# Dense–SiLU–dense on one core: first chunk by DMA transpose with the contraction outermost over eight PSUM banks, row-tiled tails, one SiLU activation

## The chip, the core and the metric

The kernel runs on one core of a Trainium2 chip. The metric is device time in microseconds (us) of one execution, median over the runs that were timed. Lower is better.

## What is computed

```python
B, S, D, F = 1, 2048, 640, 1728        # x: (B,S,D)  w1: (D,F)  w2: (F,D), all bf16
h = jnp.einsum("bsd,df->bsf", x, w1)
h = h * sigmoid(h)                     # silu
out = jnp.einsum("bsf,fd->bsd", h, w2)
```

Both products contract over the partition dimension of 128: D = 640 is five slices (`DT = 5`), F = 1728 is thirteen full slices and a tail of 64. The first product needs x transposed (D on the partitions), the second needs h with F on the partitions, which is how the first one writes it.

## The kernel before, in words

The instructions of each engine are written out by hand in their order; semaphores tie the engines together. The sequence is cut into four chunks of 512 rows (`SCH`, `NSC`).

**Getting x transposed.** Chunk 0 is loaded as it lies, half by SP (L206) and half by ACT (L401), and turned on TensorE: 20 matmuls of 128x128 against an identity that POOL builds (L184 to L196), L295, whose results VectorE and ScalarE copy from PSUM to `xT_sb` (L468, L416). Chunks 1 to 3 are transposed by the DMA engines on the way in, five transposes of 512x128 per chunk, issued by SP (L224). SP issues nothing of these before the first half of x has landed (wait ahead of L213) and the third group of w1 has landed (wait ahead of L224). w1 comes in four groups of columns (L406 on ACT, L213 on SP), w2 in four pieces on SP after chunk 2's transposes (L233, L236, L243).

**Warm-up.** TensorE multiplies zeros nine times, 512 columns each (L277), while the first data is on its way.

**First product.** A unit is one chunk by one slice of F: five matmuls of 512 columns, one for each slice of D, into one of four PSUM banks (`ps1`, L350). The first two slices of chunk 0 are split into halves of 256 columns. ScalarE writes the sigmoid of a unit to SBUF (L426), VectorE multiplies it with the unit in PSUM and writes `hT_sb` (L490). The tail of 64 columns of F is done for two chunks at a time (L339): the two matmuls of a pair write partitions 0 to 63 and 64 to 127 of one bank, and the result goes to the matching half of slice 13 of `hT_sb` (L481). POOL clears that slice first (L198), so the other half of it is zero.

**Second product.** For each of 16 tiles of 128 rows, all 14 slices of F, the 14th being the half-filled tail at full height: one matmul of 512 columns and one of 128 for each slice (L388), into two pairs of banks in turn (`ps2`). VectorE copies the 512 columns out (L503), ScalarE the 128 (L438), SP stores the tile (L259). The last two tiles are done together so that the last step is the narrow one: VectorE copies 1024 columns (L515), ScalarE 256 (L450), with stores by SP (L265) and ACT (L455).

Of the kernel before, what the change touches and what calls it, by code (L numbers as in the profile page):

```python
# [6 lines left out]
ALU = mybir.AluOpType  # L7


def bass_standalone__dense_activation_silu__prompt_kernel(  # L10
# [14 lines left out]
    assert D % P == 0 and S % 512 == 0 and 512 < D <= 1024  # L25
    DT = D // P
    FT = (F + P - 1) // P
    FP = FT * P
    F_LAST = F - (FT - 1) * P
    ST = S // P  # L30
    SCH = 512
    NSC = S // SCH
    JB = SCH // P
    NB1 = 4
    NOB = 4
    DA = 512
    DB = D - DA
    assert ST >= 4 and ST % 2 == 0 and (ST - 2) % NOB + 1 == (ST - 1) % NOB
    assert JB % 2 == 0

    w1_groups = [(0, 2), (2, 4), (4, 8), (8, FT)]
    N_W1_ACT = 1
    W1_BIG = 2

    def w1_group_of(ft):
        for gi, (a, b) in enumerate(w1_groups):
            if a <= ft < b:
                return gi
        raise AssertionError

    HN = SCH // 2
    N_SPLIT_FT = 2
    units = []
    for ft in range(N_SPLIT_FT):
        units.append((0, ft, 0, HN))
    for ft in range(N_SPLIT_FT):
        units.append((0, ft, HN, HN))
    PACK_TAIL = (F_LAST <= 64) and (FT >= 2)
    FT_REG = FT - 1 if PACK_TAIL else FT
    for ft in range(N_SPLIT_FT, FT_REG):  # L60
        units.append((0, ft, 0, SCH))
    for sc in range(1, NSC):
        for ft in range(FT_REG):
            units.append((sc, ft, 0, SCH))
        if PACK_TAIL and sc % 2 == 1:
            units.append((-1, sc - 1, sc, 0))
    if PACK_TAIL and NSC % 2 == 1:
        units.append((-1, NSC - 1, None, 0))
    NU = len(units)

    def unit_chunks(u):
        if u[0] == -1:
            return [c for c in (u[1], u[2]) if c is not None]
        return [u[0]]

    dve_incs = [len(unit_chunks(u)) if u[0] == -1 else 1 for u in units]
    dve_val = []
    acc = 0
    for inc in dve_incs:
        acc += inc  # L80
        dve_val.append(acc)
    chunk_done_cnt = {}
    for i, u in enumerate(units):
        for c in unit_chunks(u):
            chunk_done_cnt[c] = dve_val[i]
    def tail_half(sc):
        if not PACK_TAIL:
            return 0
        if NSC % 2 == 1 and sc == NSC - 1:
            return 0  # L90
        return sc % 2

    n_w2_full = FT - 1 if F_LAST != P else FT
    w2_half = n_w2_full // 2
    n_w2_dmas = (4 if (F - (FT - 1) * P) <= 64 else 3) if n_w2_full != FT else 2
    N_INIT = 3 + (1 if (not PACK_TAIL and FP != F) else 0)
    N_PAD = 1 if (PACK_TAIL or FP != F) else 0
    N_WARM_MM = 9
    TPV = 3
    assert TPV <= 4 and DT - TPV <= 4  # L100

    TP_BANKS = {0: (1, 0), 1: (1, 8), 2: (0, 8), 3: (1, 0)}

    def tp_slot(j, dt):
        which, base = TP_BANKS[j % 4]
        slot = base + dt if dt < TPV else base + 4 + (dt - TPV)
        return which, slot

    with ExitStack() as es:
# [3 lines left out]
        def ps(name, shape, dtype):  # L113
            return es.enter_context(nc.psum_tensor(name, shape, dtype))

        def sem(name):
            return es.enter_context(nc.semaphore(name))

        xT_sb = sb("xT_sb", [P, DT, S], bf16)
        w1_sb = sb("w1_sb", [P, DT, FP], bf16)  # L120
        w2_sb = sb("w2_sb", [P, FT, D], bf16)
        hT_sb = sb("hT_sb", [P, FT, S], bf16)
        sig_sb = sb("sig_sb", [P, NB1, SCH], bf16)
        o_sb = sb("o_sb", [P, NOB, D], bf16)
        x0_sb = sb("x0_sb", [P, JB, D], bf16)
        ident = sb("ident", [P, P], bf16)
        warm_sb = sb("warm_sb", [P, 32], fp32)
        z_sb = sb("z_sb", [P, SCH], bf16)
        ps1 = ps("ps1", [P, NB1, SCH], fp32)
        ps2 = ps("ps2", [P, 2, 1024], fp32)  # L130
        tp_views = [
            ps1[:, :, :].rearrange("p a (k s) -> p (a k) s", s=P),
            ps2[:, :, :].rearrange("p a (k s) -> p (a k) s", s=P),
        ]

        sem_init = sem("sem_init")
        sem_w2pad = sem("sem_w2pad")
        sem_z = sem("sem_z")
        sem_x0 = [sem(f"sem_x0_{i}") for i in range(JB // 2)]
        sem_x = [None] + [sem(f"sem_x{i}") for i in range(1, NSC)]  # L140
        sem_w1 = [sem(f"sem_w1_{i}") for i in range(len(w1_groups))]
        sem_w2 = sem("sem_w2")
        sem_o = [sem(f"sem_o{i}") for i in range(NOB)]
        sem_tp = sem("sem_tp")
        sem_tpc_v = sem("sem_tpc_v")
        sem_tpc_a = sem("sem_tpc_a")
        sem_pe1 = sem("sem_pe1")
        sem_act1 = sem("sem_act1")
        sem_dve1 = sem("sem_dve1")
        sem_pe2 = sem("sem_pe2")  # L150
        sem_ev_v = sem("sem_ev_v")
        sem_ev_a = sem("sem_ev_a")
        sem_ofin = sem("sem_ofin")
        block = es.enter_context(nc.Block())

        w1_v = w1.rearrange("(dt p) f -> p dt f", p=P)
        x0_v = xf[0:SCH, :].rearrange("(j p) d -> p j d", p=P)
        w2_full_v = w2[0:n_w2_full * P, :].rearrange("(ft p) d -> p ft d", p=P)

        segs = []  # L160
        for st in range(ST - 2):
            b2 = st % 2
            segs.append([(st, 0, b2, 0, DA), (st, 1, b2, DA, DB)])
        sA, sB = ST - 2, ST - 1
        segs.append([(sA, 0, 0, 0, DA), (sB, 0, 0, 512, DA)])
        segs.append([(sA, 1, 1, 0, DB), (sB, 1, 1, 512, DB)])
        grp_order = []
        for seg in segs:
            for g in seg:
                grp_order.append((g[0], g[1]))  # L170
        grp_idx = {g: i + 1 for i, g in enumerate(grp_order)}
        seg_done_idx = {}
        for seg in segs:
            last = max(grp_idx[(g[0], g[1])] for g in seg)
            for g in seg:
                seg_done_idx[(g[0], g[1])] = last
        grp_loc = {}
        for seg in segs:
            for (st, ci, b2, c0, ncol) in seg:
                grp_loc[(st, ci)] = (b2, c0, ncol)  # L180

        @block.gpsimd
        def _(pool):
            pool.memset(z_sb[:, SCH // 2:SCH], 0.0).then_inc(sem_z, 1)  # L184
            pool.memset(ident[:, :], 0.0).then_inc(sem_init, 1)
            pool.wait_ge(sem_init, 1)
            pool.affine_select(
                out=ident[:, :],
                in_=ident[:, :],
                compare_op=ALU.not_equal,  # L190
                fill=1.0,
                base=0,
                pattern=[[-1, P]],
                channel_multiplier=1,
            ).then_inc(sem_init, 1)
            pool.memset(warm_sb[:, :], 0.0).then_inc(sem_init, 1)  # L196
            if PACK_TAIL:
                pool.memset(hT_sb[:, FT - 1, :], 0.0).then_inc(sem_w2pad, 1)  # L198
            elif FP != F:
                pool.memset(w1_sb[:, :, F:FP], 0.0).then_inc(sem_init, 1)  # L200
                pool.memset(w2_sb[:, FT - 1, :], 0.0).then_inc(sem_w2pad, 1)

        @block.sync
        def _(sp):
            hj = JB // 2
            sp.dma_start(  # L206
                out=x0_sb[:, 0:hj, :], in_=x0_v[:, 0:hj, :]
            ).then_inc(sem_x0[0], 16)

            def load_w1_group(gi):  # L210
                a, b = w1_groups[gi]
                f0, f1 = a * P, min(b * P, F)
                sp.dma_start(  # L213
                    out=w1_sb[:, :, f0:f1], in_=w1_v[:, :, f0:f1]
                ).then_inc(sem_w1[gi], 16)

            sp.wait_ge(sem_x0[0], 16)
            for gi in range(N_W1_ACT, len(w1_groups)):
                load_w1_group(gi)

            def x_chunk_transposes(sc):
                s0 = sc * SCH
                for dt in range(DT):
                    sp.dma_start_transpose(  # L224
                        out=xT_sb[:, dt, s0:s0 + SCH],
                        in_=xf[s0:s0 + SCH, dt * P:(dt + 1) * P],
                    ).then_inc(sem_x[sc], 16)

            sp.wait_ge(sem_w1[W1_BIG], 16)
            for sc in range(1, NSC):  # L230
                x_chunk_transposes(sc)
                if sc == min(2, NSC - 1):
                    sp.dma_start(  # L233
                        out=w2_sb[:, 0:w2_half, :], in_=w2_full_v[:, 0:w2_half, :]
                    ).then_inc(sem_w2, 16)
                    sp.dma_start(  # L236
                        out=w2_sb[:, w2_half:n_w2_full, :],
                        in_=w2_full_v[:, w2_half:n_w2_full, :],
# [308 lines left out]
```

## Time and profile before

| | |
|---|---|
| runs (us) | 130.3, 190.81, 131.05; median 131.05 |
| span of the profiled execution | 128.5 us |
| own time of the profiled execution | not given apart; the two near runs lie 1.8 and 2.5 us above its span |
| busy: TensorE, VectorE, ScalarE, POOL | 124.7, 52.1, 39.5, 2.8 us |
| DMA | 9.87 MB, mean 77 GB/s over the span |

The profile shows one execution. Line numbers (L388) are lines of the kernel before. The timeline and the chain give starts and durations in us from the start of the span; groups give the count, the busy time in us and the mean duration of one in ns. Matmuls are pipelined, so the mean duration of one is longer than the distance from one to the next; distances are had by dividing a stretch by its count. PE is TensorE, PEld its weight loads, DVE VectorE, ACT ScalarE, SPq and ACTq the DMA issues of SyncE and ScalarE.

### The profile page before, as it was taken

How to read it: one execution, taken by the hardware profiler on the slowest of the kernel's cores; microseconds unless marked ns; L12 is line 12 of the kernel's file. 1: busy time of each engine (PE TensorE's matmuls, PEld its weight loads, DVE VectorE, ACT ScalarE, POOL GpSimd, SP SyncE). 2: the span in 40 equal slices, each digit the busy share in tenths (PEclk: the TensorE clock that was granted, in tenths of full speed). 3: DMA queues.
4: the chain of work that ended last, by engine and by line, in shares of the span. 5: the costliest groups of instructions: out<-in, count | busy, mean ns of one | idle time of the engine just before them, and what ended most of it. 6: DMA issues, size and time to landing. Idle time of an engine off the chain costs nothing.

```text
span 128.5 us, 1884 instructions
## 1 busy us (share of the span) xinstructions
PE 124.7 (97%) x767; PEld 63.9 (50%) x767; DVE 52.1 (41%) x78; ACT 39.5 (31%) x77; POOL 2.8 (2%) x9
## 2 busy tenths in 40 slices
PE   6999999999999999999999999999999999999992
PEld 2574444444444444444455555555555555555461
DVE  0475666666676666666662210222220122221021
ACT  4355555555555555555520000000000000000001
POOL 7000000000000000000000000000000000000000
PEclk9999999999999999999999999999999999999999
DMA  3897463599900000000000111111011111011103
GB/s 100 258 367 207 109 96 87 98 355 347 195 8 5 0 3 0 0 0 0 0 5 15 36 51 51 56 51 48 3 51 51 56 51 51 12 39 56 51 0 102
DMA packets 15752, 9.87 MB, mean 77 GB/s; under 512 B 8832, under 2 KB 15744, under 8 KB 15744
## 3 DMA queue, kind: packets, MB, share of 16 engines
q1 hardware_dynamic: 14544, 9.03, 24.8%
q10 hardware_dynamic: 1200, 0.72, 1.8%
q8 instruction: 6, 0.10, 0.3%
q14 instruction: 2, 0.02, 0.0%
HBM read 5.16 MB, written 2.62 MB: 61 GB/s over the span
## 4 chain that ended last, share of the span: by engine, by line
PE 97%; ACT 1%; POOL 0%; issue 0%; POOLq 0%
PE ps L388 47%; PE ps L350 44%; PE ps L277 3%; PE ps L339 2%; PE ps L295 1%; ACT xT_sb L416 1%; ACT o_sb L450 0%; POOL z_sb L184 0%; POOLq L532 0%
## 5 line engine op out<-in xcount | busy, mean ns | idle before, releaser
L388 PE MATMUL ps<-w_sb,hT_sb 128*128 128x512 bf16 (+1 forms) x448 | 61.0, 299 | 0.0
L350 PE MATMUL ps<-xT_sb,w_sb 128*128 128x512 bf16 (+1 forms) x270 | 56.5, 371 | 0.0
L388 PEld LDWEIGHTS ps<-w_sb,hT_sb 128*128 128x128 bf16 x448 | 34.4, 98 | 26.8 <-issue 0.4
L490 DVE TENSOR_TENSOR hT_sb<-ps,sig_sb 128x512 bf16<-128x512 f32 (+1 forms) x54 | 36.3, 672 | 19.9 <-ACT sig_sb L426 19.4
L350 PEld LDWEIGHTS ps<-xT_sb,w_sb 128*128 128x128 bf16 x270 | 26.2, 98 | 29.9 <-issue 0.4
L426 ACT ACTIVATE sig_sb<-ps 128x512 bf16<-128x512 f32 (+1 forms) x56 | 32.6, 582 | 26.5 <-PE ps L350 25.3
L503 DVE CAST o_sb<-ps 128x512 bf16<-128x512 f32 x14 | 9.7, 692 | 42.3 <-PE ps L388 42.3
L438 ACT CAST o_sb<-ps 128x128 bf16<-128x128 f32 x14 | 3.7, 266 | 49.3 <-PE ps L388 49.3
L277 PE MATMUL ps<-z_sb 128*128 128x512 bf16 x9 | 3.4, 557 | 1.1 <-POOL z_sb L184 1.1
L468 DVE CAST xT_sb<-ps 128x384 bf16<-128x384 f32 x4 | 1.9, 549 | 4.1 <-PE ps L295 4.1
L515 DVE CAST o_sb<-ps 128x1024 bf16<-128x1024 f32 x1 | 1.2, 1225 | 5.4 <-PE ps L388 5.4
L481 DVE TENSOR_TENSOR hT_sb<-ps,sig_sb 64x512 bf16<-64x512 f32 x4 | 2.8, 689 | 1.1 <-ACT sig_sb L426 1.0
L450 ACT CAST o_sb<-ps 128x256 bf16<-128x256 f32 x1 | 0.4, 373 | 7.3 <-PE ps L388 7.3
L277 PEld LDWEIGHTS ps<-z_sb 128*128 128x128 bf16 x9 | 1.1, 136 | 2.9 <-issue 1.8
L339 PE MATMUL ps<-xT_sb,w_sb 128*64 128x512 bf16 x20 | 2.5, 384 | 0.0
L416 ACT CAST xT_sb<-ps 128x256 bf16<-128x256 f32 x4 | 1.3, 373 | 1.9 <-PE ps L295 1.9
L410 ACT ACT_TABLE_LOAD x1 | 1.3, 1283 | 1.8 <-issue 1.8
L198 POOL MEMSET hT_sb<- 128x2048 bf16 x1 | 1.8, 1805 | 0.0
L339 PEld LDWEIGHTS ps<-xT_sb,w_sb 128*64 128x64 bf16 x20 | 1.0, 109 | 1.5 <-issue 0.8
L295 PE MATMUL ps<-ident,x_sb 128*128 128x128 bf16 x20 | 1.4, 219 | 0.2 <-ACT xT_sb L416 0.2
L295 PEld LDWEIGHTS ps<-ident,x_sb 128*128 128x128 bf16 x20 | 1.1, 97 | 0.8 <-issue 0.5
L463 DVE MEMSET z_sb<- 128x128 uint32 x1 | 0.2, 165 | 0.8 <-PEq L532 0.8
(9 smaller groups left out, 1.6 us busy)
## 6 DMA issues: line engine op xcount, KB each, us to landing
out_dram<-o_sb SPq DMA_DIRECT2D x14, 160.0 KB, 1.8
w_sb<-in_w_dram SPq DMA_DIRECT2D x1, 1120.0 KB, 8.1
w_sb<-in_w_dram SPq DMA_DIRECT2D x1, 960.0 KB, 5.6
w_sb<-in_w_dram SPq DMA_DIRECT2D x1, 880.0 KB, 7.2
w_sb<-in_w_dram SPq DMA_DIRECT2D x1, 640.0 KB, 5.5
x_sb<-in_x_dram SPq DMA_DIRECT2D x1, 320.0 KB, 3.7
x_sb<-in_x_dram ACTq DMA_DIRECT2D x1, 320.0 KB, 4.0
w_sb<-in_w_dram ACTq DMA_DIRECT2D x1, 320.0 KB, 4.5
```

Source lines behind the costliest of these rows:

```text
L277: pe.matmul(ps1[:, NB1 - 1, :], lhsT=z_sb[:, 0:P], rhs=z_sb[:, :], start=True, stop=True,)
L295: ins = pe.matmul(tp_views[wv][:, sl, :], lhsT=x0_sb[:, j, dt * P:(dt + 1) * P], rhs=ident[:, :], start=True, stop=True,)
L339: ins = pe.matmul(ps1[hh * 64:hh * 64 + F_LAST, buf, :], lhsT=w1_sb[:, dt, f0:f0 + F_LAST], rhs=xT_sb[:, dt, scc * SCH:(scc + 1) * SCH], s ...
L350: ins = pe.matmul(ps1[:, buf, 0:n], lhsT=w1_sb[:, dt, ft * P:(ft + 1) * P], rhs=xT_sb[:, dt, col0:col0 + n], start=(dt == 0), stop=(dt == ...
L388: ins = pe.matmul(ps2[:, b2, c0:c0 + ncol], lhsT=hT_sb[:, ft, st * P:(st + 1) * P], rhs=w2_sb[:, ft, d0:d0 + ncol], start=(ft == 0), stop= ...
L416: act.copy(out=xT_sb[:, TPV:DT, j * P:(j + 1) * P], in_=tp_views[wv][:, s0_:s0_ + (DT - TPV), :],).then_inc(sem_tpc_a, 1)
L426: act.activation(out=sig_sb[:, buf, 0:n], in_=ps1[:, buf, 0:n], func=ACT.Sigmoid,).then_inc(sem_act1, 1)
L438: act.copy(out=o_sb[:, ob, DA:D], in_=ps2[:, b2, c0:c0 + ncol]).then_inc(sem_ev_a, 1)
L468: dve.tensor_copy(out=xT_sb[:, 0:TPV, j * P:(j + 1) * P], in_=tp_views[wv][:, s0_:s0_ + TPV, :],).then_inc(sem_tpc_v, 1)
L481: dve.tensor_tensor(out=hT_sb[hh * 64:hh * 64 + F_LAST, FT - 1, scc * SCH:(scc + 1) * SCH], in0=ps1[hh * 64:hh * 64 + F_LAST, buf, :], in1 ...
L490: dve.tensor_tensor(out=hT_sb[:, ft, col0:col0 + n], in0=ps1[:, buf, 0:n], in1=sig_sb[:, buf, 0:n], op=ALU.mult,).then_inc(sem_dve1, 1)
L503: dve.tensor_copy(out=o_sb[:, ob, 0:DA], in_=ps2[:, b2, c0:c0 + ncol]).then_inc(sem_ev_v, 1)
```

## The change

All of the kernel is rewritten. In the words of the code:

- **Chunk 0** is transposed by the DMA engines like the others. SP begins with the five transposes of chunk 0, those of chunk 1 follow, then w2, then chunks 2 and 3; SP waits for nothing ahead of them. The loads of x, the identity, the transposing matmuls and their copies are gone.
- **w1** is loaded wholly by ACT: five pieces of 128 rows of D by the first 1024 columns of F, then the other 704 columns in one piece. Each piece of 1024 columns, and each transpose of chunk 0, has a semaphore of its own.
- **Start of the first product.** For chunk 0 the slices of D are outermost: when slice d of w1 and of x is there, eight matmuls for eight slices of F go into eight banks. The other units have their five matmuls together, as before, over eight banks in turn.
- **Warm-up**: twelve matmuls of 256 columns on a constant.
- **SiLU**: one ScalarE activation from PSUM to `hT` takes the place of the sigmoid, `sig_sb` and VectorE's multiply. A unit's bank comes free after ScalarE alone.
- **Tail in the second product**: it lies in a buffer of its own (`hTl`), chunk 2g on partitions 0 to 63 and chunk 2g+1 on 64 to 127. The second product goes over pairs of tiles, one of each of the two chunks, and the tail's matmuls contract over 64 partitions, two of them (one from each half) beside one another. The tails come after the first tile pair's main slices and before the next one's, so that eight tail matmuls lie together.
- **Output**: a buffer for each of the 16 tiles; the last tile alone has its 512 columns first and its 128 columns last.

The core of the diff (the removed lines are those told above):

```diff
-            sp.wait_ge(sem_x0[0], 16)
-            sp.wait_ge(sem_w1[W1_BIG], 16)
+            transposes(0)
+            transposes(1)
+            h = NF // 2
+            for a, b in ((0, h), (h, NF)):
+                sp.dma_start(
+                    out=w2_sb[:, a:b, :], in_=w2_v[:, a:b, :]
+                ).then_inc(sem_w2, 16)
...
+            for c in range(2, NC):
+                transposes(c)
...
-            for j in range(JB):
-                transpose_block(j)
+            for i in range(N_WARM):
+                pe.matmul(
+                    ps[:, NB - 1, 0:256],
+                    lhsT=ones[:, 0:P],
+                    rhs=ones[:, 0:256],
...
+            for d in range(DT):
+                need(sem_w1[d], 16)
+                need(sem_x0[d], 16)
+                for f in range(NB):
+                    ins = pe.matmul(
+                        ps[:, f, :],
+                        lhsT=w1_sb[:, d, f * P:(f + 1) * P],
+                        rhs=xT[:, d, 0:CH],
+                        start=(d == 0),
+                        stop=(d == DT - 1),
+                    )
+                    if d == DT - 1:
+                        ins.then_inc(sem_pe1, 1)
...
+            for i in range(NB, NU):
...
+                need(sem_act1, i - NB + 1)
...
+        for k, (t0, t1) in enumerate(pairs):
+            mains = []
+            for t in (t0, t1):
+                if t == LAST:
+                    mains += [(t, f, q) for q in range(2) for f in range(NF)]
+                else:
+                    mains += [(t, f, q) for f in range(NF) for q in range(2)]
+            tails = [(t, None, q) for q in range(2) for t in (t0, t1)]
+            mm2 += mains + tails if k % 2 == 0 else tails + mains
...
+                if f is None:
+                    need(sem_act1, done_at[c - c % 2, None])
+                    p0 = (c % 2) * FL
+                    j = (t % TPC) * P
+                    ins = pe.matmul(
+                        ps[:, bank, 0:cols.stop - cols.start],
+                        lhsT=hTl[p0:p0 + FL, c // 2, j:j + P],
+                        rhs=w2_sb[p0:p0 + FL, NF, cols],
...
+            for d in range(DT):
+                act.dma_start(
+                    out=w1_sb[:, d, 0:FB], in_=w1_v[:, d, 0:FB]
+                ).then_inc(sem_w1[d], 16)
+            act.dma_start(
+                out=w1_sb[:, :, FB:F], in_=w1_v[:, :, FB:F]
+            ).then_inc(sem_w1r, 16)
...
+            for i, (c, f) in enumerate(units):
+                act.wait_ge(sem_pe1, i + 1)
+                dst = hTl[:, c // 2, :] if f is None else hT[:, f, c * CH:(c + 1) * CH]
+                act.activation(
+                    out=dst, in_=ps[:, i % NB, :], func=ACT.Silu
+                ).then_inc(sem_act1, 1)
```

## The prediction

> **What bounds the kernel now.** I read the page's busy shares first, then the chain of waits that ended last in order of time.
>
> ```profile
> span 128.5 us, 1884 instructions
> PE 124.7 (97%) x767; PEld 63.9 (50%) x767; DVE 52.1 (41%) x78; ACT 39.5 (31%) x77; POOL 2.8 (2%) x9
> ```
>
> ```profile
> 1.10 3.44 PE ps L277 x9
> 4.54 0.45 PE ps L295 x5
> ...
> 6.17 28.26 PE ps L350 x140
> 34.43 1.20 PE ps L339 x10
> 35.63 28.16 PE ps L350 x130
> 63.79 1.20 PE ps L339 x10
> 64.99 60.97 PE ps L388 x448
> 125.97 0.02 issue
> 125.99 0.37 ACT o_sb L450
> ```
>
> TensorE is never left waiting from 6.17 to 125.97. So the span is four terms: 6.17 before the first useful matmul, 58.82 first product (6.17 to 64.99), 60.97 second product, 2.55 from the last matmul to the end; together 128.5. VectorE and ScalarE are far from bounding it. Only what shortens one of these four terms counts.
>
> Next the groups with shapes kept apart, for the price of one instruction:
>
> ```profile
> L426 ACT ACTIVATE sig_sb<-ps 128x512 bf16<-128x512 f32 x52 | 31.1, 597 | 25.6 <-PE ps L350 24.4 <-PE ps L339 1.2
> L490 DVE TENSOR_TENSOR hT_sb<-ps,sig_sb 128x512 bf16<-128x512 f32 x50 | 34.6, 692 | 19.2 <-ACT sig_sb L426 19.1
> L277 PE MATMUL ps<-z_sb 128*128 128x512 bf16 x9 | 3.4, 557 | 1.1 <-POOL z_sb L184 1.1
> L438 ACT CAST o_sb<-ps 128x128 bf16<-128x128 f32 x14 | 3.7, 266 | 49.3 <-PE ps L388 49.3
> L450 ACT CAST o_sb<-ps 128x256 bf16<-128x256 f32 x1 | 0.4, 373 | 7.3 <-PE ps L388 7.3
> ```
>
> A matmul of 512 columns follows the last one after 28.16/130 = 0.217 us; a pair of 512 and 128 in the second product takes 60.97/224 = 0.272. The nine of the warm-up took 3.44/9 = 0.382 each: TensorE starts at about half pace and is at full pace by 4.5 us, some 3 us after its first matmul (the granted-clock row says 9 throughout and doesn't show it; the distances do).
>
> Last SP's timeline, the landing times of the transposes' line, and busy stretches with DMA share and GB/s in the last two columns:
>
> ```profile
> 10.38 13.34 SPq L224 DMA_TRANSPOSE xT_sb<-in_x_dram  x10
> ...
> 26.23 8.14 SPq L224 DMA_TRANSPOSE xT_sb<-in_x_dram  x5
> ```
>
> ```profile
> DMA to landing us min/median/max: 2.7/3.4/7.5
> ```
>
> ```profile
> 7.00:10.00 3.00, 3.00 (x22) 2.00 (x21) 1.74 (x5) 1.82 (x5) 0.00 (x0) 1.00 1.07 380
> 13.00:25.00 12.00, 12.00 (x58) 5.40 (x56) 7.73 (x12) 6.70 (x12) 0.00 (x0) 1.00 0.50 100
> 26.00:32.00 6.00, 6.00 (x30) 2.72 (x28) 3.67 (x7) 3.42 (x6) 0.00 (x0) 1.00 1.06 365
> ```
>
> Transposes leave SP one per 1.33 us (13.34/10) and use half of the DMA engines' time (0.50), so about 0.67 us of it each: SP's issue paces them, not the engines. Plain loads run at 365 to 380 GB/s and fill the engines.
>
> **The change, term by term.**
>
> *Start (6.17 before).* The 20 transposing matmuls and their copies (4.54 to 6.17) go; in their place the first eight matmuls wait for the first piece of w1 and the first transpose. SP's first issue is at 0.74 and waits for nothing. With the median 3.4 the first transpose lands at 4.1, the others 1.33 apart, to 9.5. One pass of eight matmuls takes 8 x 0.217 = 1.73, more than 1.33, so once started TensorE is the slower one and the five passes need 8.65 without a gap. The w1 piece (0.25 MB, ACT's first issue at 0.74) takes under 1 us at 365 GB/s; the page's x half of 320 KB landed after 3.7, so it comes at about the same time. Six ACT issues of about 0.5 us end at 3.8, the table load of 1.28 at 5.1; ScalarE is needed first near 11.
>
> Clock: the warm-up's twelve matmuls of 256 columns cost 12 x 0.191 = 2.3 us at the rate of the nine, from about 0.8 to 3.1, then TensorE idles for about a microsecond. The trace has no such gap. I charge 0.4 (bounds: 0, if the clock comes up as it did; 1.5, if the first 3 us of real work run at the pace of the nine, 3.44 instead of 9 x 0.217 = 1.95). Effective start: 4.1 + 0.4 = 4.5. Bounds: 0.74 + 2.7 = 3.4, and 0.74 + 7.5 = 8.2, the worst landing, which was behind w2's loads.
>
> *First product (58.82).* Same 260 matmuls of 512 columns (the 20 of 256 were 10 of them) and the same 20 tail matmuls. VectorE's multiply goes; it was beside TensorE, so it gives nothing. The SiLU activation isn't in the trace; taken as a sigmoid (0.597), which TensorE's 5 x 0.217 = 1.08 per unit hides; from twice that (1.2) on it would bind. At the end of the d-outer block eight banks finish 0.217 apart, and ScalarE needs 0.63 for each. The ninth unit wants bank 0 when the eighth bank is done, 1.5 after bank 0 was done: ScalarE has then cleared two, and TensorE asks for one more each 1.08. No wait. Next that could be late: chunk 1's transposes, issued by 0.74 + 10 x 1.33 = 14.0 and landed near 16, wanted at 4.5 + 13 x 1.08 = 18.5. The rest of w1, ACT's sixth issue at 3.3 with the longest such landing 7.2, at 10.5, wanted at 13.1. Chunk 2's transposes stand behind w2 (four issues, 2.4 us): issued from 16.5 over 8.14, landed by about 27, wanted at 34. So 58.8 stays.
>
> *Second product (60.97).* Main slices: 16 x 13 x 0.272 = 56.6. Tails: 16 x 0.272 = 4.4 before. Now four clusters of eight matmuls, in pairs on separate halves of the rows. Nearest row: L339, where pairs on separate halves of the columns took 1.20 for ten, 0.24 per pair against 0.217 for one alone. Pairing halves 4 x 0.272 = 1.09 to 0.54 per cluster; the row's surplus over 5 x 0.217 is 0.12, and I add as much again for the weight loads of the narrow ones: about 0.75, four times 3.0. So 59.6, a gain of 1.4. Bounds: 58.8 (no surplus), 61.9 (no pairing, 0.23 lost per cluster).
>
> *End (2.55).* The last copy is 128 columns (0.266) for 256 (0.373), and its store is half as large: 2.4. The 512-column copy (0.69) and its store lie beside the 13 narrow matmuls, about 0.7. Bounds 2.2 and 2.6.
>
> Sum: 4.5 + 58.8 + 59.6 + 2.4 = 125.3, or 3.2 below the span of 128.5. The profiled execution's own time isn't given; what lies around its span is 2.55 by the median of 131.05, so I take the difference from the median: 131.05 - 3.2 = 127.9, 2.4% less.
>
> **Two rules against the trace.** The row: before, no transpose ran beside a load of the other queue; five behind w2 in the same queue took 8.14, 1.63 each against 1.33. The Trainium skill ("DMA: Bandwidth & Descriptors", Queues, rings and completion order) says that each DMA engine takes turns between the queues, one whole packet at a time. It speaks against this change, since w1 on ACT's queue now takes turns with the transposes that the first matmul waits for. With its typical packet of 9 to 17 descriptors an estimate is 0.3 us of delay, a sum of 125.6; with one-descriptor packets it is the first rival below.
>
> The row for the tails is L339's 0.12 per ten. "TensorEngine Tiling (Array Packing)", Tiling Modes, says that a change of tiling mode drains TensorE, without a price. With a drain of one matmul's latency beyond its distance (L339's 0.379 less 0.217, my estimate, twice per cluster) the tails would be 3.5 and the sum 125.8.
>
> **The rivals.**
>
> 1. *Turns one row at a time.* Sixteen engines hold, from w1, 40 rows of 2 KB (95 ns each at 365 GB/s over 16 engines at share 1.06) and 40 of 1.4 KB (65 ns); from each transpose 32 rows of 256 B (0.67/32 = 21 ns). Strictly in turn from 2.2: the first transpose is through after 32 x 116 ns, at 5.9, the next at 8.9, 10.6, 11.3, 12.0; each 0.4 later for the landing. Passes then begin at 6.3, 9.3, 11.0, 12.8, 14.5 and end at 16.2: an effective start of 7.6. Sum 7.6 + 58.8 + 59.6 + 2.4 = 128.4, no change: 131.0. For it: loads fill the engines alone (share 1.07). Against: at 26 to 32 the share passes 1, so engines overlap packets.
> 2. *Tails don't pair.* Second product 61.9: sum 127.6, or 130.1. For it: no K=64 matmul in the trace. Against: L339 pairs.
> 3. *Slower: transposes starve behind w1.* If w1's 2.2 MB goes ahead (6.0 us at 365 GB/s, from 2.1) the first transpose lands at about 9.2; TensorE has idled six microseconds and begins at half pace (1.5 more): start 10.7, sum 131.5, or 134.0. It decides, against the 128.5 of before, from an effective start of 7.7; it costs 2% from 10.3. For it: the 7.5 landing behind w2. Against: that was one queue in its order, these are two.
>
> **How the numbers follow.** Forecast 0.54, rival 1 0.19, rival 2 0.15, rival 3 0.08, other things 0.04. The forecast's own range is 126.2 (start 3.6, tails at 2.4) to 129.3. A measurement of this kernel can tell about 2% (2.6 us) from no change, that is a time below 128.4. Some 0.8 of the forecast's cases are below it, 0.43, and 0.03 of the rest: faster 0.46. Rivals 1 and 2 and the rest of the forecast are within: 0.44. Slower 0.10: rival 3 and what rival 1 does with a cold clock. The range is 126.2 to 131.5: it takes in rivals 1 and 2 and leaves out rival 3 and the tips.
>
> **What would show it.** Start: the first d-outer matmul at 4 to 4.5, the last of its 40 by about 13, with no gap between passes; rival 1 shows gaps of a microsecond after the first pass, rival 3 a first matmul after 8. A cold clock shows as 0.43 between matmuls there. First product: no idle TensorE until it ends near 63. Tails: clusters of eight at 0.6 to 0.9 us; 1.1 or more means no pairing. End: 2.4. I am wrong if a transpose beside w1's load lands later than about 6, if SiLU takes over 1.2, or if chunk 1 lands after 18.

## The result, and the profile after

The changed kernel takes 132.54 us (median of 4 runs, 131.83 to 134.01) against 130.89 of before: ratio 1.012, interval 1.0076 to 1.0164. It is about 1% slower, where 2.4% less was forecast. Ratios and their intervals leave out runs more than 1.5% above the fastest of the same kernel (here 134.01, and one of before at 190.81), while medians and spreads are of all runs. The profiled execution, the fastest of the four, took 131.83 with a span of 130.0.

The page's first two lines, then the chain that ended last in order of time (start, us, what), of the changed kernel:

```profile
span 130.0 us, 1655 instructions
...
PE 122.1 (94%) x726; PEld 60.9 (47%) x740; DVE 10.7 (8%) x16; ACT 36.5 (28%) x72; POOL 0.2 (0%) x4
```

```profile
3.30 9.23 DMA xT<-in_x_dram
12.54 0.14 issue
12.67 4.69 PE ps L180 x21
17.36 0.05 issue
17.41 0.59 PE ps L180 x2
18.01 10.14 PE ps L210 x47
...
66.80 1.20 PE ps L201 x10
68.00 1.47 PE ps L245 x10
...
75.17 0.65 PE ps L236 x8
...
122.53 5.12 PE ps L245 x37
127.65 0.02 issue
127.67 0.27 ACT o_sb L275
```

The chain no longer begins on TensorE: it goes back to a transpose of x that SP issued at 3.30 and that landed 9.23 later. The terms against the forecast:

| term | before | forecast | after |
|---|---|---|---|
| until the first 40 full matmuls (or as many) are done | 14.8 | 13.15 (4.5 + 8.65) | 18.01 |
| rest of the first product | 50.2 | 50.15 | 49.99 (18.01 to 68.00) |
| second product | 60.97 | 59.6 | 59.65 (68.00 to 127.65) |
| end | 2.55 | 2.4 | 2.3 |

Only the first is off, by 4.9. TensorE's timeline (start, us, what, in brackets the idle time before and what ended it) shows it:

```profile
4.97 3.49 PE L180 MATMUL ps<-xT,w_sb 128*128 128x512 bf16 x8 [1.48 <-DMA xT<-in_x_dram]
...
9.18 1.89 PE L180 MATMUL ps<-xT,w_sb 128*128 128x512 bf16 x8 [0.73 <-DMA xT<-in_x_dram]
...
12.67 5.34 PE L180 MATMUL ps<-xT,w_sb 128*128 128x512 bf16 x23 [1.60 <-DMA xT<-in_x_dram]
```

The passes begin at 4.97, 9.18 and 12.67 instead of 4.5, 6.2 and 8.0. The first ran at half pace (3.49 for eight, 0.43 from one to the next), and that cost nothing: it was done at 8.46, and the second transpose landed at 9.05. The issues on SP, ten transposes in 16.23 where ten took 13.34 before, the landing times of all twenty, and the DMA share and GB/s (last two columns) in the first pass and in the stretch after it:

```profile
0.73 16.23 SPq L120 DMA_TRANSPOSE xT<-in_x_dram  x10
```

```profile
DMA to landing us min/median/max: 2.9/3.9/9.5
```

```profile
4.97:8.46 3.49, 3.49 (x8) 0.99 (x8) 0.00 (x0) 0.56 (x2) 0.00 (x0) 1.00 1.09 190
8.46:12.60 4.14, 1.89 (x8) 0.71 (x8) 0.00 (x0) 0.00 (x0) 0.00 (x0) 1.00 1.10 228
```

The DMA engines are full (1.09, 1.10) but move 190 to 228 GB/s; before, loads alone moved 380 at 1.07. In the trace's DMA packets the second transpose's 512 rows of x lie between 4.54 and 7.88: 3.34 us for 32 rows per engine, or 104 ns each, where a row of x takes 18 at the median. In that time 225 rows of w1 ran as well, 171 ns each at the mean; the median of all 640 such rows is 84, and 43 of the 225 took more than 200. The landing came 1.17 after the last row.

### The profile page after: what moved, and what is told of

It reads as the page before. It is cut to its first block, busy times and chain, and to the rows that moved or that the text cites. A ratio compares the mean times of both kernels' runs of the same rounds, so it can differ in the third digit from the quotient of the medians.

```text
span 130.0 us, 1655 instructions
## 1 busy us (share of the span) xinstructions
PE 122.1 (94%) x726; PEld 60.9 (47%) x740; DVE 10.7 (8%) x16; ACT 36.5 (28%) x72; POOL 0.2 (0%) x4
## 4 chain that ended last, share of the span: by engine, by line
PE 88%; DMA 7%; SPq 2%; issue 1%; ACT 0%
PE ps L245 43%; PE ps L210 36%; DMA xT<-in_x_dram 7%; PE ps L180 4%; PE ps L236 2%; SPq L120 2%; PE ps L201 2%; ACT o_sb L275 0%
## 5 line engine op out<-in xcount | busy, mean ns | idle before, releaser
L245 PE MATMUL ps<-w_sb,hT 128*128 128x128 bf16 (+1 forms) x407 | 56.7, 297 | 0.6 <-issue 0.2
L210 PE MATMUL ps<-xT,w_sb 128*128 128x512 bf16 x216 | 47.4, 379 | 0.3 <-issue 0.2
L245 PEld LDWEIGHTS ps<-w_sb,hT 128*128 128x128 bf16 x416 | 31.8, 98 | 25.5 <-issue 1.5
L270 ACT ACTIVATE hT<-ps 128x512 bf16<-128x512 f32 x52 | 30.0, 608 | 30.7 <-PE ps L210 19.7
L210 PEld LDWEIGHTS ps<-xT,w_sb 128*128 128x128 bf16 x220 | 21.4, 98 | 26.2 <-issue 0.4
L180 PE MATMUL ps<-xT,w_sb 128*128 128x512 bf16 x39 | 10.7, 427 | 3.9 <-DMA xT<-in_x_dram 3.8
L180 PEld LDWEIGHTS ps<-xT,w_sb 128*128 128x128 bf16 x40 | 4.0, 105 | 10.5 <-issue 7.2
L168 PE MATMUL ps<-const-bfloat16-1.0 128*128 128x256 bf16 x12 | 2.7, 417 | 0.8 <-PEq L304 0.8
L236 PE MATMUL ps<-w_sb,hTl 64*128 64x512 bf16 (+1 forms) x32 | 2.9, 299 | 0.0
L201 PE MATMUL ps<-xT,w_sb 128*64 128x512 bf16 x20 | 2.5, 384 | 0.0
L168 PEld LDWEIGHTS ps<-const-bfloat16-1.0 128*128 128x128 bf16 x12 | 1.7, 144 | 1.4 <-issue 0.7
L270 ACT ACTIVATE hTl<-ps 128x512 bf16<-128x512 f32 x2 | 1.2, 597 | 1.2 <-PE ps L201 1.2
```

Source lines behind the costliest of these rows:

```text
L168: pe.matmul(ps[:, NB - 1, 0:256], lhsT=ones[:, 0:P], rhs=ones[:, 0:256], start=True, stop=True,)
L180: ins = pe.matmul(ps[:, f, :], lhsT=w1_sb[:, d, f * P:(f + 1) * P], rhs=xT[:, d, 0:CH], start=(d == 0), stop=(d == DT - 1),)
L201: ins = pe.matmul(ps[h * FL:(h + 1) * FL, b, :], lhsT=w1_sb[:, d, NF * P:F], rhs=xT[:, d, (c + h) * CH:(c + h + 1) * CH], start=(d == 0), ...
L210: ins = pe.matmul(ps[:, b, :], lhsT=w1_sb[:, d, f * P:(f + 1) * P], rhs=xT[:, d, c * CH:(c + 1) * CH], start=(d == 0), stop=(d == DT - 1),)
L236: ins = pe.matmul(ps[:, bank, 0:cols.stop - cols.start], lhsT=hTl[p0:p0 + FL, c // 2, j:j + P], rhs=w2_sb[p0:p0 + FL, NF, cols], start=(fi ...
L245: ins = pe.matmul(ps[:, bank, 0:cols.stop - cols.start], lhsT=hT[:, f, t * P:(t + 1) * P], rhs=w2_sb[:, f, cols], start=(first2[t, q] == i ...
```

## The experiments

Theories: *turns* (a transpose waits, row for row, for w1's rows in the other queue), against *slow by itself* (a transpose at the start of a run is late whatever runs beside it), and against *the rest* (SiLU, eight banks and tile pairs lose as well). Spans are of one profiled execution each.

**Start of before, rest of the change.**

```diff
-            transposes(0)
+            sp.dma_start(out=x0_sb[:, 0:2, :], in_=x0_v[:, 0:2, :]).then_inc(sem_x0[0], 16)
+            sp.wait_ge(sem_x0[0], 16)
...
+                    ins = pe.matmul(ps[:, b, k * P:(k + 1) * P],
+                        lhsT=x0_sb[:, j, d * P:(d + 1) * P], rhs=ident[:, :], start=True, stop=True)
```

> The start of the kernel before (chunk 0 loaded as it lies and turned on TensorE, the four column groups of w1), with all the rest of the changed kernel. Theory: the whole loss lies in the start, which ended its 40 matmuls at 18.0 where 13 was forecast; the second product of 59.65 and the end of 2.3 stay gained. The first useful matmul at about 6.3, span 6.3 + 58.7 + 59.65 + 2.3 = 126.9, 3 us under the changed kernel's 130.0 and 1.6 under the 128.5 of before. Rival: the rest loses too (SiLU, eight banks, pairs of tiles): span 128.5 or more.

Measured: 128.88 against 131.0, ratio 0.985 (0.9822 to 0.9878); span 127.1. TensorE's timeline of this kernel:

```profile
4.65 1.37 PE L215 MATMUL ps<-ident,x_sb 128*128 128x128 bf16 x20
6.35 2.34 PE L230 MATMUL ps<-xT,w_sb 128*128 128x256 bf16 x20 [0.32 <-DVE xT L344]
8.74 13.54 PE L261 MATMUL ps<-xT,w_sb 128*128 128x512 bf16 x61
```

Useful work from 6.35 without a gap (its warm-up has 17 matmuls instead of 12). So the rest of the change gains 1.5%, and the new start loses more than that. *The rest* is out as a cause of the loss.

**The transposes with nothing beside them.**

```diff
+            act.wait_ge(sem_x0[DT - 1], 16)
             for d in range(DT):
                 act.dma_start(
```

> ACT loads no w1 before all five transposes of chunk 0 have landed. Transposes alone: SP's pace, landed 1.3 apart, the fifth at about 9; then w1's first piece near 11.7 and passes without waits for x. Theory of turns: exactly this, 40 matmuls done at 11.7 + 8.65 = 20.4, or 22 with a cold clock. Rival, transposes are slow at the start of a run by themselves: the fifth lands at 12 or later.

Measured: span 135.0. In the trace they landed at 3.4, 4.8, 6.0, 7.4 and 8.7, 1.3 apart, each 0.45 to 0.48 after its last row for the first four: *slow by itself* is out. The passes then waited for w1 (first matmul at 11.95, after an idle of 8.47), began at about half pace (10 matmuls in 4.05 us) and ended at 23.1.

**The last piece of w1 held back.**

```diff
+            act.wait_ge(sem_x0[1], 16)
             act.dma_start(
                 out=w1_sb[:, :, FB:F], in_=w1_v[:, :, FB:F]
...
```

ScalarE's activation that loads its table moves ahead of the wait.

> ACT holds the last piece of w1 (the other 704 columns) until the second transpose has landed (9.0 us). Theory of turns: each DMA engine takes one row of one queue, then one of the other, so 32 rows of a transpose cost 32 rows of w1 as well; the third and fourth transpose stood beside the last piece (2.4 us of packets each) and now have the engines alone: landed by about 10.3 and 11.0, passes without a gap from 9.1, the 40 matmuls done by 16.1 instead of 18.0, span 128.1. The first two transposes stay at 4.8 and 9.0. Rival, transposes are slow whatever runs beside them: third at 12.5 as before, span 130 or more.

Measured: 132.29 (129.95 to 132.64, 10 runs). Six of the ten lie between 132.29 and 132.64; the other four, 129.95 to 131.86, give the ratio of 1.0007 (0.9962 to 1.0052). The profiled execution is the slowest of the ten. In it the second transpose landed at 10.0 (9.0 expected) and the other three at 10.4, 10.9 and 11.4: with w1 out of the way they are 0.5 apart, so it is w1 beside them that makes them late. But the 40 matmuls were done at 18.9, not 16.1. The busy stretches of this kernel (the third number from the end is the granted clock):

```profile
5.18:7.07 1.89, 1.89 (x8) 0.68 (x8) 0.00 (x0) 0.00 (x0) 0.00 (x0) 1.00 1.09 146
7.07:10.15 3.08, 0.00 (x0) 0.03 (x1) 0.00 (x0) 0.00 (x0) 0.00 (x0) 1.00 1.16 212
10.15:13.90 3.75, 3.75 (x10) 1.41 (x11) 0.00 (x0) 0.00 (x0) 0.00 (x0) 0.54 1.12 237
13.90:18.90 5.00, 4.95 (x24) 2.25 (x23) 0.00 (x0) 1.47 (x4) 0.00 (x0) 1.00 1.07 286
```

TensorE idled 3.08, and its clock then fell to half for 3.4 us: 32 matmuls took 18.9 - 10.15 = 8.75 instead of 32 x 0.217 = 6.94. What the freed transposes gave, the clock took back in this execution. The fastest of its runs, 129.95, had a span of 128.1, the number that was expected without the clock; that it kept the clock up fits, but isn't shown: its trace wasn't taken.

**Longer rows.** w1 in five pieces of whole rows.

```diff
-                    out=w1_sb[:, d, 0:FB], in_=w1_v[:, d, 0:FB]
+                    out=w1_sb[:, d, 0:F], in_=w1_v[:, d, 0:F]
```

> w1 in five pieces of whole rows (1728 columns, 3456 bytes) instead of 1024 columns and a rest: the same bytes, on ACT, in longer rows. Turns row for row: a row of w1 now takes about 141 ns of a DMA engine instead of 84, so a transpose beside it needs 32 x (141 + 18) ns = 5.1 us instead of 3.3, and the second pass begins near 11 instead of 9.2; once w1 is through, the last three transposes land 0.6 apart. Turns by bytes or by time: the second pass stays near 9.2.

Measured: span 134.1. The passes of this kernel:

```profile
6.45 2.68 PE L179 MATMUL ps<-xT,w_sb 128*128 128x512 bf16 x8 [2.96 <-DMA xT<-in_x_dram]
12.71 9.48 PE L179 MATMUL ps<-xT,w_sb 128*128 128x512 bf16 x31 [3.58 <-DMA xT<-in_x_dram]
```

The second pass begins at 12.71, 3.5 later than in the changed kernel's profile; then the last three landed 0.5 apart (13.0, 13.5, 14.0). Not all of the 3.5 is due to the longer rows, since this landing differs between executions: the traces of the six kernels with the changed kernel's loads and transposes (the changed kernel and five below) have the second transpose at 9.05 to 11.16, this one at 12.57. Its rows took 3.86 us (5.1 expected), no longer than in some of those six (3.24 to 4.16). It is later because its first row came at 5.94 (there 4.28 to 4.63); it landed 2.77 after its last row (there 1.17 to 2.82). Among its 512 rows ran 260 of w1, in the six 225 to 279: about as many, with 1.7 times the bytes each. That speaks against turns by bytes. One row for one row would be 512, and the second transpose shows that in none of these traces.

**All of it in one queue.**

```diff
+            for d in range(DT):
+                sp.dma_start(out=w1_sb[:, d, 0:FB], in_=w1_v[:, d, 0:FB]).then_inc(sem_w1[d], 16)
+                sp.dma_start_transpose(
+                    out=xT[:, d, 0:CH], in_=xf[0:CH, d * P:(d + 1) * P]).then_inc(sem_x0[d], 16)
+            sp.dma_start(out=w1_sb[:, :, FB:F], in_=w1_v[:, :, FB:F]).then_inc(sem_w1r, 16)
```

> w1's pieces go on SP's queue, each ahead of its transpose, the rest of w1 after the fifth; ACT loads nothing. The same bytes in one order, no turns. Theory of turns: a transpose lands some 3 us after its issue, at about 4.2, 6, 7.7, 9.5, 11.3; the passes end at 13, the ninth unit then waits for the rest of w1 until 14.8: effective start 6.2, span 126.8. Rival, transposes are slow beside any load or at the start of a run: gaps between the passes stay 3 us and more, 40 matmuls done at 17 or later, span 129.5 or more.

Measured: 130.27, ratio 0.9935 (0.9903 to 0.9966); span 127.8. TensorE's timeline of this kernel:

```profile
4.15 1.98 PE L189 MATMUL ps<-xT,w_sb 128*128 128x512 bf16 x8 [0.67 <-DMA xT<-in_x_dram]
6.32 1.89 PE L189 MATMUL ps<-xT,w_sb 128*128 128x512 bf16 x8 [0.19 <-DMA xT<-in_x_dram]
8.37 1.89 PE L189 MATMUL ps<-xT,w_sb 128*128 128x512 bf16 x8 [0.16 <-DMA xT<-in_x_dram]
10.44 3.61 PE L189 MATMUL ps<-xT,w_sb 128*128 128x512 bf16 x15 [0.18 <-DMA xT<-in_x_dram]
15.69 6.65 PE L219 MATMUL ps<-xT,w_sb 128*128 128x512 bf16 x30 [1.64 <-DMA w_sb<-in_w_dram]
```

The same bytes on the same engines, in one order: passes 2.1 apart with gaps under 0.2 after the first, and at full pace. The rows of each of the first four transposes took 0.9 to 1.5 us, with 42 to 80 rows of w1 among them, and it landed 0.47 to 0.50 after its last row. The wait that was expected for the rest of w1 is there (1.64). Then that piece was cut in two:

```diff
+            FM = FB + 2 * P
+            sp.dma_start(out=w1_sb[:, :, FB:FM], in_=w1_v[:, :, FB:FM]).then_inc(sem_w1m, 16)
+            sp.dma_start(out=w1_sb[:, :, FM:F], in_=w1_v[:, :, FM:F]).then_inc(sem_w1r, 16)
```

> As the run with all of w1 on SP's queue, but the rest of w1 in two pieces, the first with the two slices of F that are wanted first; warm-up 14 instead of 12. There the 40 matmuls were done at 14.0 and the next unit waited 1.6 for the rest. Theory: that wait goes, 40 done at 14.0 and no gap after, span 14.0 + 50.0 + 59.65 + 2.3 = 126.0, 2.5 under the 128.5 of before and 1.1 under the start of before with the rest of the change. Rival, the wait moves on to the second piece or to chunk 1's transposes: 127 or more.

Measured: 127.96 (127.56 to 128.2) against 130.79, ratio 0.9784 (0.9759 to 0.9808); span 126.4. This kernel beats the one before and the one with the start of before (0.985).

```profile
4.21 7.89 PE L194 MATMUL ps<-xT,w_sb 128*128 128x512 bf16 x32 [0.30 <-DMA xT<-in_x_dram]
12.33 1.89 PE L194 MATMUL ps<-xT,w_sb 128*128 128x512 bf16 x7 [0.22 <-DMA xT<-in_x_dram]
14.28 9.89 PE L226 MATMUL ps<-xT,w_sb 128*128 128x512 bf16 x45
```

Its DMA share and GB/s over the passes (last two columns):

```profile
4.20:14.28 10.08, 9.73 (x40) 3.91 (x41) 0.00 (x0) 1.54 (x4) 0.00 (x0) 1.00 1.04 240
```

Over the same stretch the changed kernel moved 227 GB/s at a share of 1.09. The engines are hardly faster here; what changed is the order in which the bytes come.

With the first piece of w1 on ACT again:

```diff
+            act.dma_start(out=w1_sb[:, 0, 0:FB], in_=w1_v[:, 0, 0:FB]).then_inc(sem_w1[0], 16)
```

> The same, with the very first piece of w1 issued by ACT, so that SP's first transpose is issued 0.45 earlier and all behind it too. One piece of eight rows per DMA engine is all that takes turns with transposes. Theory: the first pass at about 4.2 as before (w1's first piece decides), the later passes 0.4 earlier, 40 done at 13.6, span 125.6. Rival, any turn costs: no better than the kernel with all on SP.

Measured: 128.44, ratio 0.981 (0.9784 to 0.9835); span 126.1. The interval overlaps the one above: the two can't be told apart, and the earlier issue brought nothing that shows in the time.

**TensorE kept busy in the waits.**

```diff
+                if d < 2:
+                    for _ in range(8):
+                        pe.matmul(ps[:, NB - 1, :], lhsT=z_sb[:, 0:P], rhs=z_sb[:, :], start=False, stop=False)
```

> The changed kernel with eight matmuls of zeros (which add nothing) after each of the first two passes and 18 instead of 12 in the warm-up: TensorE stays busy while it waits for transposes. Theory: transposes land as late as before, the second pass near 9.2 to 10 and the third near 12.6; but the clock no longer falls to half pace in the waits, so that no run has the 8.75 for 32 matmuls that some showed: 40 done at 18.0 in every run, times together near 131.8 where the changed kernel's runs went from 131.8 to 134.0. Rival, the clock has no part: spread and median (132.5) as before.

Measured: 132.94 (132.17 to 135.09), ratio 1.0151 (1.012 to 1.0183): a miss. The profiled execution is the slowest of the seven. In it the waits were longer than the zeros, so the clock fell all the same (0.65 in the second row), and the second set of zeros, which ran until 15.95, itself held up the third pass, whose transpose had landed at 12.63. It doesn't tell how much of the changed kernel's spread is the clock's.

```profile
8.60:10.86 2.26, 0.00 (x0) 0.03 (x1) 0.00 (x0) 0.00 (x0) 0.00 (x0) 1.00 1.08 135
10.86:13.65 2.79, 2.79 (x9) 1.14 (x10) 0.00 (x0) 0.00 (x0) 0.00 (x0) 0.65 1.06 312
```

**The d-outer order undone alone.**

```diff
-            for d in range(DT):
+            for f in range(NB):
+                for d in range(DT):
                 need(sem_w1[d], 16)
                 need(sem_x0[d], 16)
-                for f in range(NB):
```

> Chunk 0 with the contraction innermost, as the other chunks: the first unit needs all five transposes. All else is the changed kernel. Theory: the first useful matmul waits for the fifth transpose at about 14.5, the clock is at half pace by then (1.7 us more), span 14.5 + 1.7 + 58.7 + 59.65 + 2.3 = 136.9: the d-outer order itself is worth 5 to 7 us of the changed kernel. Rival: passes gain nothing, as the last transpose decides both: 133 or less.

Measured: span 136.7, as expected, 6.7 above the changed kernel's profiled execution. Some of it is the execution and not the order: its fifth transpose landed at 15.4, there at 14.5. Against the changed kernel's four spans, 130.0 to 132.1, the d-outer order is worth 4.6 to 6.7 with such a start.

**Sigmoid and multiply again.**

```diff
-                    out=dst, in_=ps[:, i % NB, :], func=ACT.Silu
+                    out=sig_sb[:, i % NB, :], in_=ps[:, i % NB, :], func=ACT.Sigmoid
...
+                dve.tensor_tensor(out=dst, in0=ps[:, i % NB, :], in1=sig_sb[:, i % NB, :], op=ALU.mult)
```

> Sigmoid on ScalarE and the multiply on VectorE, as before, in place of the one SiLU activation; all else is the changed kernel. Theory: hidden under TensorE's 1.08 per unit either way, the stretch from the end of the 40 matmuls to the start of the second product stays 50.0. Rival, the single activation shortens the path by which banks come free: 51 or more here.

Measured: span 130.9, of which the stretch from the 40th matmul to the second product is 50.14 (18.80 to 68.94), against 49.99. VectorE does 36 us more, all of it hidden.

**The tails in another order, and apart.**

```diff
-            tails = [(t, None, q) for q in range(2) for t in (t0, t1)]
+            tails = [(t, None, q) for t in (t0, t1) for q in range(2)]
```

> The four tail matmuls of a pair of tiles in another order, both of one half of the rows first, so that neighbours mostly share their half and cannot run beside one another. Theory: pairing is what brings the tails from 1.09 to 0.65 us per cluster of eight; here about 1.1, the second product 1.3 to 1.8 us longer. Rival: the gain is not from running beside one another but from the lower height of 64: second product unchanged at 59.65.

Measured: ratio 1.0168 (1.0104 to 1.0232) with the changed kernel's start; each cluster takes 0.65 as before, the second product 59.67. The rival's number came, but the run doesn't bear on its reason: the order changed nothing. The trace shows the starts within a cluster: 0 and 7 ns for the 512-column matmuls of the two halves, 226 and 233 for the narrow ones. Each half of the rows runs through its own matmuls, also when the program has both of one half first. So the tails were really put apart:

```diff
+                    mm2 += [(t, f, q) for f in [*range(NF), None] for q in range(2)]
```

> The tails of a tile after its own main slices, so that no tail of one half of the rows lies beside one of the other half; the start is that of the changed kernel and only the second product is read. Theory: alone, a tail of height 64 takes as long as one of 128 (0.272 per tile), and each switch costs 0.1: second product 56.6 + 16 x 0.37 = 62.5 instead of 59.65, longer than the 60.97 of before. Rival, the lower height is cheaper in itself: below 60.5.

```profile
73.14 0.37 PE ps L234 x2
73.52 3.64 PE ps L243 x26
77.16 0.38 PE ps L234 x2
```

Measured: the second product takes 64.55 (69.51 to 134.06). A tail alone costs 0.37 instead of 0.272, and the 26 matmuls after it 3.64 instead of 13 x 0.272 = 3.54. A height of 64 in itself saves nothing here; alone it is dearer. The gain is from running beside one another, with few switches: four clusters, not sixteen.

## Why the prediction was wrong

- *Start*: this is the step that failed. It said "SP's issue paces them, not the engines", took the median landing of 3.4 for the first transpose and let the others follow 1.33 apart. By that they land at 4.1, 5.4 and 6.8; in the trace they landed at 4.83, 9.05 and 12.54. The rows used for the price were of transposes that ran when the w1 loads were over. The half share of the DMA engines (0.50) was read as room; it was the share of a queue that had the engines alone. Against the run with the transposes alone, where the second landed at 4.83, its 4.2 us of lateness have three parts: its first row came 1.2 later (4.54 for 3.36), its rows took 2.3 longer (3.34 for 1.01), and it landed 1.17 after its last row instead of 0.45, which is 0.7. With w1 in the same queue and in the order of need the loss became a gain, so w1's rows running beside the transposes, and not in the order of need, are the cause. Two signs that the prediction named came: a transpose landed after 6, and chunk 1's last one after 18 (at 18.6; it was wanted only near 23.4).
- *Rival 1* had the right cause, w1's rows in the other queue, but neither the size nor quite the mechanism: its passes were to end at 16.2, they ended at 18.0 in the profiled execution, and the second, third and fourth transposes had 225, 138 and 476 rows of w1 among their 512, not one for one. It reckoned w1's rows at 95 ns; under both kinds of traffic 80 of the 640 long rows took more than 200 ns each, and the engines moved 190 GB/s instead of 365. It also put 0.4 from the last row to the landing, which took 0.7 to 1.8 for the first four. With it the sum was 128.4, the measured span 130.0. Its chance of 0.19 was too low: the trace before could not show two queues sharing the engines with transposes among them, and half of the chance had gone to the case that assumed they would not.
- Turns between the queues are there in the trace: w1's rows run among the transposes'. That is what the Trainium skill says ("DMA: Bandwidth & Descriptors", Queues, rings and completion order). How many rows make a turn, no run here shows: 225 rows of w1 are 14 per engine for 32 of x. The prediction's 0.3 us, estimated from the page's packet of 9 to 17 descriptors, was wrong in itself. Worked out from the same figure, 32 rows of x are two to four packets, and with one packet of w1 for each (9 to 17 rows of 95 ns, 0.9 to 1.6 us) the estimate is about 3 us, as much as row for row.
- *Clock*: priced at 0.4, with a bound of 1.5 for the first pass. That pass took 3.49 for 8 x 0.217 = 1.74, 1.75 more, but it cost nothing here, as the second transpose was later still. Where a wait for the second let the clock fall, it cost 1.8 (8.75 - 6.94). The Trainium skill's "TensorE: Matmul & The Clock Gate", Part 1, puts the fall after an idle window of about 3.4 us; in the kernel with the zeros an idle 2.26 was enough for a granted clock of 0.65 in the next stretch.
- *First product, second product, end*: right to 0.2. The SiLU activation is hidden as forecast, 0.608 a piece (the mean in ns behind the busy time) against 1.08 per unit:

```profile
L270 ACT ACTIVATE hT<-ps 128x512 bf16<-128x512 f32 x52 | 30.0, 608 | 30.7 <-PE ps L210 19.7 <-PE ps L180 11.0
```

  The tails were forecast at 0.75 per cluster and take 0.65; the 26 matmuls after them take 3.64 where 13 x 0.272 = 3.54, so the 0.75 holds for both together:

```profile
104.93 0.65 PE ps L236 x8
105.58 3.64 PE ps L245 x26
```

  *Rival 2* (no pairing) and *rival 3* (transposes starve wholly) did not come: the first transpose landed while w1 was loading.
- The range (126.2 to 131.5) ended half a microsecond above rival 1's 131.0; the time lies 1.0 above it, since rival 1 was itself sized too small.

What stays open: how the engines take turns, why the landing comes so long after the last row, and why plain rows stall when transposes run beside them. In the kernel before none of the 640 rows of 1408 bytes took more than 200 ns, in the changed kernel 70 did. Of w1's 2 KB rows about an eighth did, in two queues (80 of 640, 14 of them before the first row of x) and in one (76 of 640). One queue doesn't take the stalls away; fewer of w1's rows run among a transpose's, and it lands sooner after them. Not tested: whether it takes one queue, or whether it would do to spread w1's loads on ACT; on SP's queue their issues were also spread over more than 9 us instead of 3.3.

## What to carry to other kernels

A transfer's landing time is a price for the company it was measured in: before moving a latency-bound transfer ahead of bulk loads, ask which rows will stand beside it in the other queue. When several small pieces gate the first work, put all of them on one queue in the order of need, and cut the bulk so that what is wanted next comes first; here that turned 1.2% lost into 2.2% gained. Where an early wait lasts some 2 us or more, price the clock too: it can take back what an earlier transfer gives.

## What was not expected of the hardware

Two matmuls of height 64 on different halves of the rows started 7 ns apart even with another matmul of the first half between them in the program (3 to 4 ns where they were neighbours): in these clusters each half kept only its own order. And a wait of 2.26 us brought the clock down, while the changed kernel's profiled execution, with waits of 0.73 and 1.60, kept it up. The length of the wait alone doesn't settle it: the changed kernel's first pass ran at half pace after a wait of 1.48, that of the kernel with w1's last piece held back at full pace after 1.69.
